# Linear attention and a tanh-shrink MLP on one core: the key sums spread over DRAM, and the last denominators on VectorE

## The chip, the cores and the metric

The kernel runs on one core of a Trainium2 chip. The metric is the device time of one execution in microseconds (us). Three runs of the kernel before took 283.5, 283.87 and 283.98 us; the median is 283.87 us.

The core has five engines that run beside each other and meet at semaphores: TensorE (PE, with its weight loads shown as PEld), VectorE (DVE), ScalarE (ACT), GpSimd (POOL) and SyncE (SP, which here only issues transfers). Each engine works through its own instructions in the order in which the program issued them. Transfers (DMA) are issued by SP or by POOL and are moved by 16 DMA engines.

## The reference: what is computed

There are 8 batches, 8 heads, 576 tokens and 64 numbers per head. All arrays are float32.

```
phi(x) = where(x > 0, x, exp(x) - 1) + 1
kv  = sum over tokens of phi(k) v        (64 x 64 for each batch and head)
z   = sum over tokens of phi(k)          (64 numbers for each batch and head)
num = phi(q) kv
den = phi(q) . z + 1e-6
x   = num / den                          -> 4608 tokens x 512
h   = x w_in                             (512 x 2048)
g   = h - tanh(h)
out = g w_out                            (2048 x 512)
```

## The kernel before, in words

**Chunks.** The MLP runs over nine chunks `c` of 512 tokens. Chunk 0 to 7 holds the first 512 tokens (eight of nine groups of 64) of batch `c`; chunk 8 holds the ninth group of all batches, the "last tokens". A chunk has two parts. In the first (`l1mm`, L458) 16 steps `fi` of 4 matmuls make h, into PSUM bank `fi % 6`; after every odd step ACT takes tanh of two banks (`l1act2`, L464) and DVE subtracts it from h into `gT` (L465), which frees the two banks. So step 6 of a chunk can't write bank 0 before the DVE subtraction of steps 0 and 1 is done. In the second part (`l2mm`, L479) 16 steps `s` of 4 matmuls make the output, four steps for 128 tokens; ACT copies each result to one of five `osb` buffers (L490), and SP stores it in two or four transfers (L503).

**Attention in the gaps.** While chunk `c` is computed, the attention of the batches `n1 = c + 1` and `n2 = c + 2` is prepared. The order is written out by hand: `s1[i]` lists what is issued after step `i` of the first part, `s2[i]` what is issued after step `i` of the second part. What is in a list is put into the engines' queues at that place, whether its inputs are ready or not.

**Batches 3 to 7** (`n2 >= QS`) take this way. In `s2` of chunk `c`, ACT and DVE make phi(k) and phi(q) of batch n2. At `s2[9]` (`s2[12]` in chunk 1) `a_num` computes the numerators of batch n1 and then, with 72 small matmuls (L198), kv and z of batch n2. z comes out with one number on each of 128 partitions (two heads of 64) for four pairs of heads. It is needed the other way round: all 64 numbers along the free dimension, on all partitions. For this `kz_copy` has DVE copy z, repeated 64 times, to `zr` (L218); two steps later `q_zb` multiplies `zr` with the identity on PE (L227, two matmuls), and ACT copies the product to `zb` (L230). POOL multiplies phi(q) with `zb` in two halves `i` (`q_prod`, L237), and DVE sums each half and head (`q_den`, L242, four reductions): the first half is summed at `s2[15]` of the same chunk (in chunk 2 at `s1[2]` for batch 3), the second at `s1[3]` and `s1[5]` of the next. At `s1[7]` `q_scale` adds 1e-6 and inverts on DVE, POOL scales phi(q) (L251), and SP issues a transposing transfer (L170) whose result `a_num` uses.

**The last tokens of batches 0 and 1** are left out of the load of q in those batches. They are loaded in chunk 3 (`load_qr`), go through phi in chunk 4 (`r_phi`, which also issues their transposition, L327), and at `s2[9]` of chunk 6 `r_den` makes their denominators on PE (L335), DVE inverts them (L338, L340), SP takes them through DRAM to all partitions (L343, L347), and `r_num` makes the numerators on PE (L288). In chunk 7 `r_scale` divides on DVE (L359).

**Loads.** `load_k`, `load_q` and `load_v` of the batch after n2 are issued by POOL at `s2[9]` (in chunk 1 at `s2[15]`), in this order; k and q have one buffer each, v has two.

Of the kernel before, what the change touches and what calls it, by code (L numbers as in the profile page):

```python
# [18 lines left out]
def kernel(  # L19
# [115 lines left out]
    zr_t, zb_t, pr_t, dn_t, r_t = {}, {}, {}, {}, {}  # L135
# [76 lines left out]
    def kz_copy(b, b0, o):  # L212
        ps = ps_all[:, b0:b0 + 2, o:o + 132].rearrange("p g (i e) -> p g i e", i=2)
        if b < QS:
            nc.vector.tensor_mul(kz_t[b][:, :, :, 64:96], ps[:, :, :, 64:65].to_broadcast([128, 2, 2, 32]), mask)
        else:
            zr_t[b] = rpool.tile([128, 2, 2, 64], BF16, name="zr")
            nc.vector.tensor_copy(zr_t[b].rearrange("p i g t -> p g i t"),  # L218
                                  ps[:, :, :, 64:65].to_broadcast([128, 2, 2, 64]))
        nc.vector.tensor_copy(kz_t[b][:, :, :, 0:64], ps[:, :, :, 0:64])  # L220


    def q_zb(b, bank):

        ps = ps_all[:, bank, 0:256]
        for i in range(2):
            nc.tensor.matmul(ps[:, 128 * i:128 * i + 128], zr_t[b][:, i].rearrange("p g t -> p (g t)"), ident,  # L227
                             start=True, stop=True)
        zb_t[b] = rpool.tile([128, 2, 128], BF16, name="zb")
        nc.scalar.copy(zb_t[b].rearrange("p i x -> p (i x)"), ps)  # L230
# [87 lines left out]
    def r_phi():  # L318
# [6 lines left out]
        nc.vector.tensor_tensor(y, e, r, ALU.min)  # L325
        qT_t["r"] = const.tile([128, 2, 2, 2, 64], BF16, name="qTr")
        nc.sync.dma_start_transpose(out=qT_t["r"].rearrange("p b i g t -> p (b i) (g t)"), in_=y)  # L327

    def r_den(bank, o):

        qT = qT_t["r"]
        ps = ps_all[0:64, bank, o:o + 64]
        for n, p in enumerate((0, 2, 1, 3)):
            for b in range(2):
                nc.tensor.matmul(ps[32 * b:32 * b + 32], kz_t[b][:, p // 2, p % 2, 64:96], qT[:, b, p % 2, p // 2, :],  # L335
                                 start=(n == 0), stop=(n == NP - 1))
        den = const.tile([64, 64], F32, name="denr")
        nc.vector.tensor_scalar(den, ps, 1e-6, None, ALU.add)  # L338
        rden = const.tile([64, 64], F32, name="rdenr")
        nc.vector.reciprocal(rden, den)  # L340
        ds = dram.tile([2, H, 64], F32, name="dsr")
        for b in range(2):
            nc.sync.dma_start(out=ds[b], in_=rden[32 * b:32 * b + H])  # L343
        rdb = rdb_t["r"] = const.tile([128, 2, NP, 64], F32, name="rdbr")
        for b in range(2):
            for hh in range(2):
                nc.sync.dma_start(  # L347
                    out=rdb[64 * hh:64 * hh + 64, b].rearrange("p a t -> p (a t)"),
                    in_=ds[b, 4 * hh:4 * hh + 4].rearrange("a t -> (a t)").partition_broadcast(64))

    def r_num(b0, o):

        pr_t["r"] = [rest_mm(b, b0, o + 128 * b, qT_t["r"][:, b].unsqueeze(2)) for b in range(2)]

    def r_scale():

        for b in range(2):
            for h, ps in enumerate(pr_t["r"][b]):
                nc.vector.tensor_mul(xT[:, 2 * h:2 * h + 2, rest_at(b):rest_at(b) + 64], ps,  # L359
                                     rdb_t["r"][:, b, 2 * h:2 * h + 2])  # L360
# [123 lines left out]
    def evac(c, i, o, f0=0, f1=None):  # L484
# [145 lines left out]
    for c in range(NC):  # L630
# [4 lines left out]
        if c == 0:  # L635
# [44 lines left out]
            def k2(i):  # L680
                ks.append(phi_pieces(2, k_t, kp_t, "kp", i))
                ks[i][1]()
# [3 lines left out]
        elif n1 < B:  # L686
            if c == 1:
# [15 lines left out]
            if c == 3:  # L703
                s1[12].append(load_qr)
            if c == 4:
                s2[1].append(r_phi)
            if c == B - 2:
                s2[m].append(lambda: (r_den(7, 384), r_num(6, 128)))
            s2[m].append(lambda: a_num(n1, n2 if n2 < B else 0))
            if n2 < B:  # L710
                s2[m + 2].append(lambda: (q_zb(n2, 4 if c == 1 else 7), q_prod(n2)))
                if c > 1:
                    s2[15].append(lambda: (q_den(n2, 0, 0), q_den(n2, 0, 1)))
        if c == B - 1:
            s1[3].append(r_scale)
        if c == 1:
            for i in range(2):
                s1[1 + 2 * i].append(lambda i=i: ks[i][0]())
                s1[3 + 2 * i].append(lambda i=i: ks[i][2]())
            s1[0].append(lambda: (a_vp(2, 0, nc.gpsimd), a_vp(2, 1, nc.gpsimd),  # L720
                                  gate(qT_t[n1]), load_k(n2), load_q(n2), load_v(n2)))
        if c >= 1 and n2 < B:
# [7 lines left out]
            if n2 + 1 < B:  # L730
                s2[15 if c == 1 else 9].append(lambda: (load_k(n2 + 1), load_q(n2 + 1), load_v(n2 + 1)))
# [91 lines left out]
```

## Time and profile before

| | |
|---|---|
| median of three runs | 283.87 us |
| the profiled execution's own time | 283.29 us |
| its span, first to last instruction | 281.5 us |
| PE busy | 276.1 us, 98% of the span |
| DVE, ACT, POOL busy | 176.9, 146.0, 81.9 us |
| granted TensorE clock | 1.00 |
| transfers | 33.25 MB in 40135 packets, mean 118 GB/s |

Busy time is the time in which an engine worked on instructions. The chain is the work that ended last, followed back from the last instruction: each piece of it is what the next one waited for. What stands on the chain costs time, and what does not stand on it is covered. Of the chain 91% is PE, above all the two big matmul lines L458 (43%) and L479 (41%).

### The profile page before, as it was taken

The numbers are of one execution on the slowest core, as the hardware profiler recorded it, in microseconds if no ns is written. First come the engines' busy times: TensorE is split into PE (matmuls) and PEld (weight loads), VectorE is DVE, ScalarE is ACT, GpSimd is POOL, SyncE is SP. The second block draws the span as 40 slices with busy tenths as digits, with TensorE's granted clock in tenths as the row PEclk, the third lists the DMA queues.
The fourth block names the chain that finished last, engine by engine and source line by source line (L and its number), as shares of the span: only waits on it lengthen the run. The fifth ranks groups of instructions, "written<-read, shape, count | busy, mean of one in ns | idle before, by whom it ended". The sixth has DMA issues, their size and how long they took to land.

```text
span 281.5 us, 5103 instructions
## 1 busy us (share of the span) xinstructions
PE 276.1 (98%) x2085; PEld 131.0 (47%) x2085; DVE 176.9 (63%) x285; ACT 146.0 (52%) x177; POOL 81.9 (29%) x79
## 2 busy tenths in 40 slices
PE   8899999999999999999999999999999999999995
PEld 3574544444544454445444544454444444444443
DVE  5759967993879755976398839763961177006600
ACT  4747918856255654675357636673541365126411
POOL 8642330320092434362623361406050000000000
PEclk9999999999999999999999999999999999999999
DMA  6999999799829899079904990342025210230023
GB/s 102 189 205 207 205 207 206 158 196 213 228 46 204 117 199 214 1 123 161 207 18 96 173 222 18 73 90 67 8 43 118 77 36 2 51 78 20 2 66 83
DMA packets 40135, 33.25 MB, mean 118 GB/s; under 512 B 17744, under 2 KB 35824, under 8 KB 39984
## 3 DMA queue, kind: packets, MB, share of 16 engines
q0 software_dynamic: 18688, 18.35, 41.5%
q1 hardware_dynamic: 21424, 14.58, 21.9%
q8 instruction: 16, 0.26, 0.3%
q14 instruction: 7, 0.06, 0.0%
HBM read 38.14 MB, written 9.46 MB: 169 GB/s over the span
## 4 chain that ended last, share of the span: by engine, by line
PE 91%; DMA 4%; DVE 1%; ACT 1%; issue 1%; POOL 1%; SPq 0%; DVEq 0%; POOLq 0%
PE ps_all L458 43%; PE ps_all L479 41%; DMA out_dram<-osb 3%; DMA kraw<-in_k_dram 2%; PE ps_all L198 2%; PE ps_all L742 1%; PE ps_all L279 1%; ACT osb L490 1%; SPq L503 0%; PE ps_all L309 0%; POOL qraw L101 0%; ACT e L151 0%; PE ps_all L182 0%; PE ps_all L371 0%; DVE rden L380 0%
## 5 line engine op out<-in xcount | busy, mean ns | idle before, releaser
L479 PE MATMUL ps_all<-w_out_sb,gT 128*128 128x512 bf16 x560 | 124.6, 379 | 0.0
L458 PE MATMUL ps_all<-xT,w_in_sb 128*128 128x512 bf16 x560 | 122.8, 379 | 0.0
L465 DVE TENSOR_TENSOR gT<-ps_all,th 128x1024 bf16<-128x1024 f32 x64 | 77.7, 1217 | 45.2 <-ACT th L464 45.2
L464 ACT ACTIVATE th<-ps_all 128x1024 f32<-128x1024 f32 x64 | 65.6, 1024 | 46.7 <-PE ps_all L458 46.7
L458 PEld LDWEIGHTS <-w_in_sb 128*128 128x128 bf16 x560 | 54.6, 98 | 65.7 <-issue 0.3
L479 PEld LDWEIGHTS <-gT 128*128 128x128 bf16 x560 | 53.8, 98 | 63.2 <-issue 0.2
L490 ACT COPY osb<-ps_all 128x512 f32<-128x512 f32 (+1 forms) x36 | 20.7, 582 | 56.9 <-PE ps_all L479 46.3
L237 POOL TENSOR_TENSOR pr<-qp,zb 128x1152 f32<-128x1152 bf16 x10 | 23.4, 2359 | 37.8 <-ACT zb L230 37.8
L251 POOL TENSOR_TENSOR qp<-qp,rd 128x1152 bf16<-128x1152 bf16 x10 | 21.0, 2115 | 36.9 <-issue 23.7
L242 DVE TENSOR_REDUCE dn<-pr 128x9 f32<-128x576 f32 x20 | 14.5, 746 | 12.2 <-POOL pr L237 12.2
L151 ACT ACTIVATE e<-qraw 128x1152 bf16<-128x1152 bf16 (+1 forms) x16 | 18.2, 1135 | 3.6 <-DMA qraw<-in_q_dram 3.6
L151 ACT ACTIVATE e<-kraw 128x1152 bf16<-128x1152 bf16 x15 | 17.5, 1165 | 0.0
L153 DVE TENSOR_TENSOR kp<-e,r 128x1152 bf16<-128x1152 bf16 x15 | 11.9, 792 | 4.1 <-ACT e L151 3.2
L153 DVE TENSOR_TENSOR qp<-e,r 128x1152 bf16<-128x1152 bf16 (+1 forms) x16 | 11.9, 742 | 4.0 <-ACT e L151 3.0
L568 PE MATMUL ps_all<-zero 128*128 128x512 bf16 x29 | 9.2, 475 | 1.2 <-DVE zero L513 1.2
L124 POOL DMA_DIRECT2D w_out_sb<-in_moe_w_out_dram x10 | 6.4, 637 | 10.1 <-DMA w_in_sb<-in_moe_w_in_dram 4.7
L104 POOL DMA_DIRECT2D kraw<-in_k_dram x7 | 5.5, 783 | 11.0 <-ACT e L151 10.6
L202 DVE COPY vp<-v 128x1152 bf16<-128x1152 bf16 x11 | 6.0, 542 | 4.0 <-DMA v<-in_v_dram 4.0
L470 DVE TENSOR_TENSOR gT<-ps_all,th 128x512 bf16<-128x512 f32 x12 | 7.9, 686 | 0.6
L104 POOL DMA_DIRECT2D qraw<-in_q_dram x7 | 5.3, 752 | 9.9 <-ACT e L151 5.2
L469 ACT ACTIVATE th<-ps_all 128x512 f32<-128x512 f32 x12 | 7.2, 596 | 1.9 <-DVE gT L748 1.0
L420 ACT CAST xT<-ps_all 128x1024 bf16<-128x1024 f32 x5 | 5.1, 1012 | 5.1 <-PE ps_all L288 4.4
(108 smaller groups left out, 146.8 us busy)
## 6 DMA issues: line engine op xcount, KB each, us to landing
out_dram<-osb SPq DMA_DIRECT2D x65, 128.0 KB, 2.4
kraw<-in_k_dram POOLq DMA_DIRECT2D x7, 576.0 KB, 7.0
qraw<-in_q_dram POOLq DMA_DIRECT2D x6, 576.0 KB, 8.7
v<-in_v_dram POOLq DMA_DIRECT2D x6, 576.0 KB, 12.4
w_in_sb<-in_moe_w_in_dram POOLq DMA_DIRECT2D x3, 512.0 KB, 9.8
v<-in_v_dram POOLq DMA_DIRECT2D x4, 288.0 KB, 8.7
rdb<-ds SPq DMA_DIRECT2D x2, 576.0 KB, 5.7
w_out_sb<-in_moe_w_out_dram POOLq DMA_DIRECT2D x4, 256.0 KB, 11.7
```

The costliest lines, as they stand in the source:

```text
L104: nc.gpsimd.dma_start(out=t[:, :, :, 0:n].rearrange("q h i j d -> q (h i) (j d)"), in_=x.rearrange("(n q) x -> q n x", n=4))
L151: return (lambda: nc.scalar.activation(e, x, AF.Exp), lambda: nc.vector.tensor_scalar(r, x, 0.0, 1.0, ALU.max, ALU.add), lambda: nc.vector ...
L153: lambda: nc.vector.tensor_tensor(y, e, r, ALU.min))
L237: nc.gpsimd.tensor_mul(pr_t[b][:, i].rearrange("p j h d -> p j (h d)"), qp_t[b][:, i].rearrange("p j h d -> p j (h d)"), zb_t[b][:, i].uns ...
L242: nc.vector.tensor_reduce(dn_t[b][:, i, :, h], pr_t[b][:, i, :, h, :], mybir.AxisListType.X, ALU.add)
L251: nc.gpsimd.tensor_mul(x, x, rd[:, i].unsqueeze(2).to_broadcast([128, J * 2, D]))
L458: nc.tensor.matmul(h, w_in_sb[:, p, fi * 128:(fi + 1) * 128], xT[:, p, c * 512:(c + 1) * 512], start=(n == 0), stop=(n == NP - 1))
L464: nc.scalar.activation(th, h, AF.Tanh)
L465: nc.vector.tensor_sub(gT[:, fi:fi + 2, :], h, th)
L479: nc.tensor.matmul(o, gT[:, fi, i * 128:(i + 1) * 128], w_out_sb[:, fi, :], start=(fi == 0), stop=(fi == NF - 1))
L490: nc.scalar.copy(osb[:, f0:f1], o[:, f0:f1])
L568: nc.tensor.matmul(ps_all[:, 0, :], zero[:, 0:128], zero, start=True, stop=True)
```

## The change

For batches 3 to 7 `zr` and the two matmuls are gone. DVE copies z as it is (four numbers a partition) to `zs`, and the new `z_rows` has SP store them to DRAM, turned round, and load them back to 128 partitions by two transfers, each to 64 partitions; these three transfers are issued by `kz_copy`, two steps before the place where `q_zb` stood. The reductions of the first half go to `s1[0]` and `s1[1]` of the next chunk (`s1[2]` and `s1[3]` in chunk 2).

For the last tokens of batches 0 and 1, z is taken from the masked columns of `kz_t` by a maximum (`r_z`, chunk 3) and goes through `z_rows` too; in chunk 4 (`r_scale`) DVE multiplies, sums, inverts and scales phi(q) before its transposition. `r_den` and the transfers of its result are gone, `r_num` writes the finished numbers, and `r_copy` copies them.

Besides: the second half of batch 2's r piece (`ks[1][1]`) moves from the end of chunk 0 to `s1[5]` of chunk 1; `kv2` and `a_den` of batch 2 go one step later; v is loaded before q; and only one instead of five of the output stores of chunk 3 is cut in two.

```diff
         if b < QS:
             nc.vector.tensor_mul(kz_t[b][:, :, :, 64:96], ps[:, :, :, 64:65].to_broadcast([128, 2, 2, 32]), mask)
         else:
-            zr_t[b] = rpool.tile([128, 2, 2, 64], BF16, name="zr")
-            nc.vector.tensor_copy(zr_t[b].rearrange("p i g t -> p g i t"),
-                                  ps[:, :, :, 64:65].to_broadcast([128, 2, 2, 64]))
+            zs = rpool.tile([128, 1, 2, 2], BF16, name="zs")
+            nc.vector.tensor_copy(zs[:, 0], ps[:, :, :, 64])
+            zb_t[b] = z_rows(zs, rpool, "zb")[:, 0]
         nc.vector.tensor_copy(kz_t[b][:, :, :, 0:64], ps[:, :, :, 0:64])
-    def q_zb(b, bank):
-        ps = ps_all[:, bank, 0:256]
-        for i in range(2):
-            nc.tensor.matmul(ps[:, 128 * i:128 * i + 128], zr_t[b][:, i].rearrange("p g t -> p (g t)"), ident,
-                             start=True, stop=True)
-        zb_t[b] = rpool.tile([128, 2, 128], BF16, name="zb")
-        nc.scalar.copy(zb_t[b].rearrange("p i x -> p (i x)"), ps)
+    def z_rows(zs, pool, name):
+        nb = zs.shape[1]
+        zd = dram.tile([nb, 2, 2, 128], BF16, name="zd" + name)
+        nc.sync.dma_start(out=zd.rearrange("n g i x -> x (n g i)"), in_=zs.rearrange("x n g i -> x (n g i)"))
+        zb = pool.tile([128, nb, 2, 128], BF16, name=name)
+        for g in range(2):
+            nc.sync.dma_start(out=zb[64 * g:64 * g + 64].rearrange("p n i x -> p n (i x)"),
+                              in_=zd[:, g].rearrange("n i x -> n (i x)").partition_broadcast(64))
+        return zb
...
+    def r_z():
+        zs = const.tile([128, 2, 2, 2], BF16, name="zsr")
+        for b in range(2):
+            nc.vector.tensor_reduce(zs[:, b], kz_t[b][:, :, :, 64:72], mybir.AxisListType.X, ALU.max)
+        zb_t["r"] = z_rows(zs, const, "zbr")
+    def r_scale():
+        y = qp_t["r"]
+        pr = const.tile([128, 8, D], F32, name="prr")
+        nc.vector.tensor_mul(pr.rearrange("p n d -> p (n d)"), y, zb_t["r"].rearrange("p b i x -> p (b i x)"))
+        dn = const.tile([128, 8], F32, name="dnr")
+        nc.vector.tensor_reduce(dn, pr, mybir.AxisListType.X, ALU.add)
+        nc.vector.tensor_scalar(dn, dn, 1e-6, None, ALU.add)
+        rd = const.tile([128, 8], F32, name="rdr")
+        nc.vector.reciprocal(rd, dn)
+        x = y.rearrange("p (n d) -> p n d", d=D)
+        nc.vector.tensor_mul(x, x, rd.unsqueeze(2).to_broadcast([128, 8, D]))
         qT_t["r"] = const.tile([128, 2, 2, 2, 64], BF16, name="qTr")
         nc.sync.dma_start_transpose(out=qT_t["r"].rearrange("p b i g t -> p (b i) (g t)"), in_=y)
-    def r_den(bank, o):
...
     def r_num(b0, o):
-        pr_t["r"] = [rest_mm(b, b0, o + 128 * b, qT_t["r"][:, b].unsqueeze(2)) for b in range(2)]
-    def r_scale():
...
+        for b in range(2):
+            rest_mm(b, b0, o + 128 * b, qT_t["r"][:, b].unsqueeze(2))
+    def r_copy(b0, o):
+        for h, copy in enumerate((nc.vector.tensor_copy, nc.scalar.copy)):
+            copy(xT[:, 2 * h:2 * h + 2, rest_at(0):rest_at(2)].rearrange("p i (b t) -> p b i t", b=2),
+                 ps_all[:, b0 + h, o:o + 256].rearrange("p (b i t) -> p b i t", b=2, i=2))
...
-                cuts = [f0, 256, f1] if c == 3 and 2 * i + half > 2 else [f0, f1]
+                cuts = [f0, 256, f1] if c == 3 and 2 * i + half > 6 else [f0, f1]
...
                 ks.append(phi_pieces(2, k_t, kp_t, "kp", i))
-                ks[i][1]()
+                if not i:
+                    ks[i][1]()
...
-                s1[10].append(kv2)
+                s1[11].append(kv2)
-                s1[12].append(lambda: (a_den(n1, 6), a_spread(n1)))
+                s1[13].append(lambda: (a_den(n1, 6), a_spread(n1)))
-                if c == 2:
-                    s1[2].append(lambda: (q_den(n1, 0, 0), q_den(n1, 0, 1)))
                 e = 2 * (c == 2)
+                for h in range(2):
+                    s1[e + h].append(lambda h=h: q_den(n1, 0, h))
...
+                s2[13].append(r_z)
             if c == 4:
                 s2[1].append(r_phi)
-            if c == B - 2:
-                s2[m].append(lambda: (r_den(7, 384), r_num(6, 128)))
-            s2[m].append(lambda: a_num(n1, n2 if n2 < B else 0))
+                s2[12].append(r_scale)
+            s2[m].append(lambda: (c == B - 2 and r_num(6, 128), a_num(n1, n2 if n2 < B else 0),
+                                  c == B - 2 and r_copy(6, 128)))
             if n2 < B:
-                s2[m + 2].append(lambda: (q_zb(n2, 4 if c == 1 else 7), q_prod(n2)))
-                if c > 1:
-                    s2[15].append(lambda: (q_den(n2, 0, 0), q_den(n2, 0, 1)))
-        if c == B - 1:
-            s1[3].append(r_scale)
+                s2[m + 2].append(lambda: q_prod(n2))
...
-                s1[3 + 2 * i].append(lambda i=i: ks[i][2]())
+                s1[3 + 2 * i].append(lambda i=i: (i and ks[i][1](), ks[i][2]()))
...
-                s2[15 if c == 1 else 9].append(lambda: (load_k(n2 + 1), load_q(n2 + 1), load_v(n2 + 1)))
+                s2[15 if c == 1 else 9].append(lambda: (load_k(n2 + 1), load_v(n2 + 1), load_q(n2 + 1)))
```

More of the change, by code (lines that the diff above doesn't have):

```diff
@@ L134 @@
     kp_t, qp_t, qT_t, kz_t, rdb_t, rden_t = {}, {}, {}, {}, {}, {}
-    zr_t, zb_t, pr_t, dn_t, r_t = {}, {}, {}, {}, {}
+    zb_t, pr_t, dn_t, r_t = {}, {}, {}, {}
     def phi_pieces(b, src, store, name, i, parts=0):
@@ L325, in r_phi @@
         nc.vector.tensor_tensor(y, e, r, ALU.min)
+        qp_t["r"] = y
+    def r_z():
[14 more added lines that the diff above has]
+        nc.vector.tensor_mul(x, x, rd.unsqueeze(2).to_broadcast([128, 8, D]))
@@ L326, in r_phi @@
         qT_t["r"] = const.tile([128, 2, 2, 2, 64], BF16, name="qTr")
         nc.sync.dma_start_transpose(out=qT_t["r"].rearrange("p b i g t -> p (b i) (g t)"), in_=y)
-    def r_den(bank, o):
[L331 to L341, printed above, removed]
-        for b in range(2):
[L343 to L349, printed above, removed]
@@ L351, in r_num @@
-    def r_num(b0, o):
-        pr_t["r"] = [rest_mm(b, b0, o + 128 * b, qT_t["r"][:, b].unsqueeze(2)) for b in range(2)]
-    def r_scale():
[L357 to L360, printed above, removed]
+    def r_num(b0, o):
+        for b in range(2):
+            rest_mm(b, b0, o + 128 * b, qT_t["r"][:, b].unsqueeze(2))
```

## The prediction

> **What bounds the kernel now.** I read the page's busy times first, then the chain in order of time, then the timeline around one batch's z, then SP's own waits, and last the transfers of that stretch.
>
> ```profile
> PE 276.1 (98%) x2085; PEld 131.0 (47%) x2085; DVE 176.9 (63%) x285; ACT 146.0 (52%) x177; POOL 81.9 (29%) x79
> ```
>
> PE has no slack. The chain shows what the change can take off it:
>
> ```profile
> 100.86 0.64 PE ps_all L198 x72
> 101.50 1.83 PE ps_all L479 x8
> 103.34 0.11 PE ps_all L227 x2
> 103.45 3.45 PE ps_all L479 x16
> 106.90 13.81 PE ps_all L458 x64
> ...
> 216.75 0.24 PE ps_all L335 x8
> 216.99 0.02 issue
> 217.01 0.23 DVE denr L338
> 217.24 0.04 issue
> 217.28 0.32 PE ps_all L288 x15
> ```
>
> The columns are start, duration, what. L227 (z spread by matmul) costs 0.11 us a batch. At 216.75 eight matmuls make r_den, and then PE waits 0.29 us for DVE to read them. L458 runs at 13.81/64 = 0.216 us a matmul, so a step of four takes 0.863.
>
> Chunk 2's timeline (start, duration, engine, line; in brackets the idle time before and what ended it):
>
> ```profile
> 101.57 0.42 DVE L218 CAST zr<-ps_all 128x256 bf16<-128x256 f32 x1 [0.58 <-PE ps_all L198]
> ...
> 103.86 0.38 ACT L230 CAST zb<-ps_all 128x256 bf16<-128x256 f32 x1
> 104.32 4.68 POOL L237 TENSOR_TENSOR pr<-qp,zb 128x1152 f32<-128x1152 bf16 x2 [2.34 <-ACT zb L230]
> 106.71 1.42 DVE L242 TENSOR_REDUCE dn<-pr 128x9 f32<-128x576 f32 x2 [3.05 <-POOL pr L237]
> ...
> 109.72 1.23 DVE L465 TENSOR_TENSOR gT<-ps_all,th 128x1024 bf16<-128x1024 f32 x1 [1.60 <-ACT th L464]
> ```
>
> DVE already stands 3.05 us for POOL's product, but before it is needed for gT; 1.60 us of idle time are left after the sums. Whatever makes zb later first eats that cover and then holds gT, the PSUM banks and PE.
>
> SP's waits for the two trips through DRAM that the kernel has (total, times, longest), and the transfers issued from 98 to 103 us and from 103 to 107 us (us to landing last):
>
> ```profile
> SPq L403 <- DMA ds<-rden: 3.7, 1, 3.7
> ...
> SPq L347 <- DMA dsr<-rdenr: 0.6, 1, 0.6
> ```
>
> ```profile
> qraw<-in_q_dram POOLq DMA_DIRECT2D x1, 576.0 KB, 8.6
> v<-in_v_dram POOLq DMA_DIRECT2D x1, 576.0 KB, 12.3
> ```
>
> ```profile
> out_dram<-osb SPq DMA_DIRECT2D x2, 128.0 KB, 6.3
> ```
>
> A few KB to DRAM kept SP 3.7 us when batch loads were under way (L403, 67.5 us) and 0.6 us when none were (L347, 219 us). An output store lands after 2.2 us at the least, but after 6.3 us here beside q and v. In chunks 2, 3 and 4 the loads run over just the place where z now takes its trip; in chunk 5 there are none, and in chunk 1 they are issued later.
>
> **The change, part by part.**
>
> *PE work removed.* Five times L227: 5 x 0.11 = 0.55. r_den 0.24 and the wait behind it 0.29: 0.53. Together 1.08 us off the chain; nothing is added on PE.
>
> *z through DRAM, chunks 2 to 5.* How late may zb be? z is out of PSUM at 101.57 + 0.2 (estimate; the 64-element DVE read L338 took 0.22) = 101.77. L458 begins at 106.79 (0.11 earlier), and its step 6 wants bank 0 after 6 x 0.863 = 5.18, at 111.97. DVE now has one reduction (L242, 0.74) queued ahead of the first gT (1.22); with 0.1 to release PE, POOL's first half must end by 109.9. It takes 2.36 + 0.08, so zb must be there by 107.5: the trip may take 5.7 us.
>
> The trip: the store, 0.1 for SP's wait, 0.53 until the second load's issue (L347's own spacing), and that load's landing. Without loads under way: store 2.4 (64 rows of 2 KB; lowest 1.24, from dsr's issue at 217.84 to L347 at 219.08; highest 4.7, a qT transposition, which is also made of small pieces), load 2.5 (rdbr). Sum 5.5: inside 5.7, so chunk 5 costs 0, up to 2.1 by the highest.
>
> With loads under way (chunks 2, 3, 4): the lowest store is ds, issued at 63.34 and waited for until 67.52, 4.2; the highest is 7.7, the maximum of the output stores. I take 4.7, near ds, which carries as little, with 0.5 for 512 separate pieces of 2 bytes instead of 8 rows. For the load the ends are 2.5 (the batch loads are through by then) and 5.7 (rdb); I take 3.5, because v now starts some 3 us earlier and the queue is nearly empty five us after the store. Trip 4.7 + 0.1 + 0.53 + 3.5 = 8.8, stall 8.8 - 5.7 = 3.1 each, 9.3 for three. The ends: 4.2 and 2.5 give 7.3, stall 1.6, 4.8 in all; 7.7 and 5.7 give 14.0, 8.3 each, 25 in all.
>
> *Chunk 1 (batch 3).* z is ready at 75.4; the first sum stands at s1[2], behind gT of steps 0 and 1, so the limit is step 8: 77.69 + 6.9 = 84.6, less 1.22 + 0.74 + 0.1 + 2.44 gives zb by 80.1, a trip of 4.7. The output stores of 73.54 and 74.05 are still in front (3.5 each); store 2.9, so 2.9 + 0.1 + 0.53 + 2.5 = 6.0: stall 1.3 (0 to 3).
>
> *What queues behind.* SP: 18 transfers come, 6 of r_den's go, and 4 cuts go. While SP waits for a store it holds the output stores issued after s2[11]; five osb buffers, refilled every 4 steps (3.45), cover that, and ACT waits for osb only in the last chunk. POOL: q_prod waits for zb; behind it stand q_scale's products, which sat idle 7.9 us before (L251), and in chunk 1 batch 4's loads, some 4 us later, with k wanted at 94. The transposition, issued at 121.12 and landed 5.5 later, was 2.7 us ahead of its use at 129.35. All these I cost at 0; if a cover is short, the next thing late is qT, and with it a_num.
>
> *Last tokens.* r_z is two reductions of some 0.16 (L617) in chunk 3. r_scale is 0.7 + 0.75 + 0.17 + 0.3 + 0.7, about 2.6 on DVE (L153, L242, L246, L248), in chunk 4 at s2[12], where DVE stood 3.05 for POOL: hidden, and its z is a chunk old. Its transposition took SP 1.23 and moves about 10 us later, still nearly two chunks ahead of use. r_copy, about 0.4 each on DVE and ACT, lies before a DVE idle of 6.76 (226.25); four L359 of 0.28 go from chunk 7. All 0, since none is on the chain and these idles cover them.
>
> *Batch 2.* kv2 one step later puts kz_copy behind one more gT; before, kz was ready about when a_den began (59.47), and I reckon 0.4 (0 to 0.9) of PE wait. rdb also comes one step later, toward the multiply at 75.94: inside that 0.4. The half r piece (0.46) only changes place on DVE.
>
> *Sum.* -1.08 + 9.3 + 0 + 1.3 + 0.4 = +9.9 us. The profiled execution's own time was 283.29 (span 281.5 and 1.8 around it), so it would be 293.2; the median of the three runs lies 0.58 higher, and I give the forecast on it: 283.87 + 9.9 = 293.8.
>
> **Two rules of the Trainium skill weighed.** The rows give 2.2 to 7.7 us for a store. "DMA: Bandwidth & Descriptors", section "Anatomy of one DMA", makes a small transfer cost about 2.0 us fixed; two in a row would be 4.0 plus issue, inside the limit, and the sum would be no stall. The rows of this case under load contradict it, so I go by them. The granted clock is 1.00 in every chunk here. "TensorE: Matmul & The Clock Gate", section "What's actually happening", halves the clock after an idle window of about 3.4 us; by that rule stalls of 3.1 would add nothing, longer ones up to some 1.7 each, about 5 for three.
>
> **Rivals.**
>
> *In time after all (faster).* SP's packets pass the batch loads: a trip under load of 5.7 or less costs nothing. For it: ds was issued as 4 transfers behind 4 slow output stores, so its 4.2 may be queue, not load. Against it: even 4.2 + 0.63 + 2.5 is 7.3. Price: -1.08 + 0 to 0.4, 282.8 to 283.2. It turns at 5.7 us.
>
> *Pieces take turns (much slower).* Each DMA engine writes 512/16 = 32 pieces; if each lets one packet of a batch load pass (1152 B; about 0.1 us: the transfers view counts some 340 packets of the loads between 105 and 107 us, on 16 engines), a store takes 3.4 more, the three stalls 6.5 each: +20 instead of +9.3, about 304.
>
> *The trip is hidden for most batches.* One stall remains: about 284 to 287.
>
> **How the numbers follow.** Forecast (three stalls) 0.65, own range 288 to 301 from the trip's ends, cut where both ends would have to meet in every batch. In time 0.18, of which 0.16 is below 283.3. Pieces take turns 0.11. One stall or less 0.06, half of it within 0.2%. So faster 0.16, same 0.06, slower 0.78, where 0.2% (0.57 us) is about what a measurement tells from no change. The range, 282.7 to 301, must reach down to the first rival to leave no more than 2 in 10 out.
>
> **What would show it.** Right: a new PE idle before step 6 of chunks 3, 4 and 5, ended by DVE gT; DVE L242 waiting for POOL pr some 6 us instead of 3; POOL waiting for a DMA into zb; no such idle in chunk 6. Wrong: zb landing within 5.7 us under load, or the sums' wait staying inside idle time. The prediction fails most easily in the landing time of a 512-piece store beside the batch loads, which no row shows.

## The result, and the profile after

The changed kernel takes 367.09 us (median of six runs, 365.72 to 370.12), beside 283.76 us for the kernel before, run next to it (six runs, 283.5 to 284.4). The ratio is 1.295, with a 95% interval of 1.290 to 1.300: 83.3 us more. The forecast was 293.8 us, its range 282.7 to 301. The direction was right and the size far out. The profiled execution took 365.72 us, its span is 363.9 us, and its mean granted clock 0.906. Runs more than 1.5% above the fastest run of the same kernel count as slow and are left out of the times and ratios below, three of four of "z by matmul" and two of five of "busy stall", whose traces are of slow runs.

The page of the kernel after, engines, slices and granted clock:

```profile
PE 281.4 (77%) x2037; PEld 132.3 (36%) x2067; DVE 177.7 (49%) x287; ACT 144.7 (40%) x173; POOL 82.3 (23%) x79
...
PE   8899999985089930999309975089952999999996
...
PEclk9999999999579995899858999579995899999999
```

The work is nearly the same as before, on every engine. PE's idle time went from 281.5 - 276.1 = 5.4 us to 363.9 - 281.4 = 82.5 us, and the slices show where: five holes of one to two slices (9.1 us each), and in each of them and just behind it a lower clock.

The waits of the kernel after (engine, line, what it waited for: us in total, times, longest):

```profile
POOL pr L238 <- DMA zb<-zdzb: 131.2, 5, 38.5
DVE dn L243 <- POOL pr L238: 94.3, 5, 22.3
...
PE ps_all L458 <- DVE gT L465: 69.5, 5, 15.6
...
PE ps_all L280 <- DMA qT<-qp: 2.6, 1, 2.6
```

Read from the top, this is the path the prediction named: POOL's product waits for `zb`, the reduction L243 waits for POOL, `gT` stands behind the reduction on DVE, and PE stands for `gT`. But the last link costs 69.5 us and not 10.6 (9.3 and 1.3). The chain of the kernel after gives one whole turn of it, from chunk 2 into chunk 3 (start, us, what):

```profile
120.11 17.44 DMA zdzb<-zs
137.62 3.39 DMA zb<-zdzb
141.00 0.62 issue
141.62 2.36 POOL pr L238
144.01 0.75 DVE dn L243
144.76 1.14 DVE gT L465
145.94 1.01 PE ps_all L458 x2
```

One KB on its way to DRAM takes 17.44 us, 32 KB back to 64 partitions 3.39. The same store has no load to compete with in chunk 5, and is still on the chain with 13.60. That chunk's timeline (start, us, engine, line; in brackets the idle time before and what ended it):

```profile
258.35 0.40 SPq L226 DMA_DIRECT2D zdzb<-zs  x1
...
271.96 1.12 SPq L229 DMA_DIRECT2D zb<-zdzb  x2
...
275.23 4.69 POOL L238 TENSOR_TENSOR pr<-qp,zb 128x1152 f32<-128x1152 bf16 x2 [26.77 <-DMA zb<-zdzb]
277.62 0.76 DVE L243 TENSOR_REDUCE dn<-pr 128x9 f32<-128x576 f32 x1 [17.64 <-POOL pr L238]
...
279.56 1.01 PE L458 MATMUL ps_all<-xT,w_in_sb 128*128 128x512 bf16 x2 [11.00 <-DVE gT L465]
```

The transfers of the kernel after (out<-in, queue, times, KB each, median us from issue to landing) have it for all of them; `zdzbr` is the trip of the last tokens:

```profile
zb<-zdzb SPq DMA_DIRECT2D x10, 32.0 KB, 3.4
...
zdzb<-zs SPq DMA_DIRECT2D x5, 1.0 KB, 17.2
zdzbr<-zsr SPq DMA_DIRECT2D x1, 2.0 KB, 16.0
```

So the load behaves as expected and the store doesn't. Why it takes 13 to 17 us, and how much of the 83 us hangs on that, is what the runs had to settle.

### The profile page after: what moved, and what is told of

It is laid out like the page before. It is cut to its first block, busy times and chain, and to the rows that moved or that the text cites. A ratio compares the mean times of both kernels' runs of the same rounds, so it can differ in the third digit from the quotient of the medians.

```text
span 363.9 us, 5043 instructions
## 1 busy us (share of the span) xinstructions
PE 281.4 (77%) x2037; PEld 132.3 (36%) x2067; DVE 177.7 (49%) x287; ACT 144.7 (40%) x173; POOL 82.3 (23%) x79
## 4 chain that ended last, share of the span: by engine, by line
DMA 44%; PE 40%; DVE 5%; POOL 3%; ACT 3%; SPq 2%; issue 2%; POOLq 0%; ACTq 0%
DMA zdzb<-zs 22%; PE ps_all L458 19%; PE ps_all L479 19%; DMA zdzbr<-zsr 4%; DMA v<-in_v_dram 4%; DMA qraw<-in_q_dram 4%; DMA zb<-zdzb 3%; DVE gT L465 3%; DMA w_in_sb<-in_moe_w_in_dram 3%; POOL pr L238 3%; DMA qT<-qp 2%; DMA out_dram<-osb 2%; ACT e L151 1%; SPq L503 1%; SPq L229 1%
## 5 line engine op out<-in xcount | busy, mean ns | idle before, releaser
L458 PE MATMUL ps_all<-xT,w_in_sb 128*128 128x512 bf16 x550 | 130.6, 395 | 72.2 <-DVE gT L465 69.5
L479 PE MATMUL ps_all<-w_out_sb,gT 128*128 128x512 bf16 x541 | 121.8, 379 | 1.7 <-issue 1.1
L458 PEld LDWEIGHTS <-w_in_sb 128*128 128x128 bf16 x560 | 56.5, 101 | 144.2 <-issue 84.5
L243 DVE TENSOR_REDUCE dn<-pr 128x9 f32<-128x576 f32 x20 | 14.9, 747 | 94.3 <-POOL pr L238 94.3
L151 ACT ACTIVATE e<-kraw 128x1152 bf16<-128x1152 bf16 x15 | 17.4, 1163 | 0.0
L153 DVE TENSOR_TENSOR kp<-e,r 128x1152 bf16<-128x1152 bf16 x15 | 11.9, 797 | 4.0 <-ACT e L151 3.1
L153 DVE TENSOR_TENSOR qp<-e,r 128x1152 bf16<-128x1152 bf16 (+1 forms) x16 | 11.9, 742 | 4.0 <-ACT e L151 3.0
L420 DVE CAST xT<-ps_all 128x1024 bf16<-128x1024 f32 x5 | 6.1, 1217 | 7.0 <-PE ps_all L289 7.0
## 6 DMA issues: line engine op xcount, KB each, us to landing
qraw<-in_q_dram POOLq DMA_DIRECT2D x6, 576.0 KB, 13.8
```

The source lines that it names most:

```text
L151: return (lambda: nc.scalar.activation(e, x, AF.Exp), lambda: nc.vector.tensor_scalar(r, x, 0.0, 1.0, ALU.max, ALU.add), lambda: nc.vector ...
L153: lambda: nc.vector.tensor_tensor(y, e, r, ALU.min))
L243: nc.vector.tensor_reduce(dn_t[b][:, i, :, h], pr_t[b][:, i, :, h, :], mybir.AxisListType.X, ALU.add)
L420: copy(xT[:, 2 * h:2 * h + 2, m:m + 512], ps_all[:, 2 * h:2 * h + 2, :])
L458: nc.tensor.matmul(h, w_in_sb[:, p, fi * 128:(fi + 1) * 128], xT[:, p, c * 512:(c + 1) * 512], start=(n == 0), stop=(n == NP - 1))
L479: nc.tensor.matmul(o, gT[:, fi, i * 128:(i + 1) * 128], w_out_sb[:, fi, :], start=(fi == 0), stop=(fi == NF - 1))
```

## The experiments

Two theories of the store stood against each other. The first counts: a transfer pays for each of its 512 writes of 2 bytes. The second looks at where they go: "turned round" means that neighbouring partitions write neighbouring 2 bytes, and pieces that share a short stretch of DRAM wait for each other. Beside them stood the question whether the store is the whole of the loss.

### The store by itself

```diff
+    trip(f"turned{r}", [4, 128], lambda d: d.rearrange("y x -> x y"), z4, ...)
+    trip(f"rows{r}", [128, 4], lambda d: d, z4, ...)
+    trip(f"one{r}", [1, 128], lambda d: d.rearrange("y x -> x y"), chain[:, 0:1], ...)
+    trip(f"apart64{r}", [4, 128, 32], lambda d: d[:, :, 0:1].rearrange("y x o -> x y o"), ...)
+    trip(f"apart512{r}", [4, 128, 256], lambda d: d[:, :, 0:1].rearrange("y x o -> x y o"), ...)
+    trip(f"wide64{r}", [4, 128, 32], lambda d: d.rearrange("y x o -> x y o"), ...)
+    trip(f"four{r}", [4, 128], lambda d: d, chain[0:4, 0:128], ...)
```

> The store by itself, without the kernel: transfers one after the other, each issued when the one before has landed, no loads. 512 pieces of 2 bytes turned round as in the change; 128 rows of 8 bytes; 128 pieces of 2 bytes; 512 pieces of 2 bytes each into its own 64 or its own 512 bytes of DRAM; 512 pieces of 64 and of 256 bytes; 4 rows of 256 bytes; 512 pieces of 2 bytes from SBUF to SBUF; the transposition of 128 x 256. Theory A1 (each small write to DRAM is completed before the next of its engine, some 0.37 us each): turned about 13 us, one about 4.5, apart 64 and 512 also 13, wide 256 well under. Theory A2 (writes into the same 64 bytes wait for each other): turned 13, apart 64 or 512 about 2.5 to 4. Either way rows, four, SBUF to SBUF and transposition about 2 to 3.

The transfers of this kernel, with nothing else under way:

```profile
zdapart<-chain SPq DMA_DIRECT2D x4, 1.0 KB, 1.8
...
zdturned<-chain SPq DMA_DIRECT2D x2, 1.0 KB, 12.8
...
zdrows<-chain SPq DMA_DIRECT2D x2, 1.0 KB, 3.0
...
zdone<-chain SPq DMA_DIRECT2D x2, 0.2 KB, 16.0
...
sb<-chain SPq DMA_DIRECT2D x2, 1.0 KB, 2.0
```

`zdturned` is the store of the change: 12.8 us alone, so competition is not needed. `zdapart` writes the same 512 pieces of 2 bytes, 64 or 512 bytes apart, in 1.8 us. `zdone` has a quarter of the pieces, side by side, and takes longer. Four rows of 256 bytes (`four`) took 1.1, and 512 pieces of 64 or 256 bytes (`wide`) 1.8 to 1.9. The first theory falls. It is not the source either: the same four numbers a partition written to SBUF (`sb`) take 2.0.

### How near is too near

```diff
+    for step in (2, 4, 8, 16, 32):                       # 4, 8, 16, 32, 64 bytes apart
+        trip(f"step{step}x{r}", [4, 128, step], lambda d: d[:, :, 0:1].rearrange("y x o -> x y o"), ...)
+    for n in (4, 16):                                    # each partition its own 64 bytes, n pieces of 2 bytes in it
+        trip(f"own{n}x{r}", [128, 1, 32], lambda d: d[:, 0, 0:n], ...)
+    trip(f"turned{r}", [4, 128, 1], ...)                 # 512 pieces side by side
+    trip(f"half{r}", [2, 128, 1], ...)                   # 256
+    trip(f"eight{r}", [8, 128, 1], ...)                  # 1024
```

> The store by itself again, no kernel around it. 512 pieces of 2 bytes with 4, 8, 16, 32 and 64 bytes from one to the next; 128 times 4 and 128 times 16 pieces of 2 bytes, where each partition's pieces lie in 64 bytes of its own; and 256, 512 and 1024 pieces side by side. In the first measurement 512 pieces side by side took 12.8 to 14.3 us, the same pieces 64 or 512 bytes apart 1.8 to 2.0, and 128 pieces side by side 16. Theory A2 (pieces in the same 64 bytes wait for each other, some 0.4 us each): 32, 16, 8, 4, 2 and 1 pieces share 64 bytes at steps of 2, 4, 8, 16, 32 and 64 bytes, so 13, 7, 4, 2.5, 2 and 2 us; the own ones 3 and 8; the number of pieces side by side hardly matters. If the stretch is larger than 64 bytes, the times at 32 and 64 differ; if smaller, those at 16 and 32 are equal.

The transfers of this kernel (the trace puts `zd` before each name, so `own4` stands as `zdown4`):

```profile
zdstep2x<-chain SPq DMA_DIRECT2D x2, 1.0 KB, 8.6
...
zdstep4x<-chain SPq DMA_DIRECT2D x2, 1.0 KB, 4.1
...
zdstep8x<-chain SPq DMA_DIRECT2D x2, 1.0 KB, 2.7
...
zdstep16x<-chain SPq DMA_DIRECT2D x2, 1.0 KB, 2.0
...
zdstep32x<-chain SPq DMA_DIRECT2D x2, 1.0 KB, 1.9
...
zdown4x<-chain SPq DMA_DIRECT2D x2, 1.0 KB, 3.4
...
zdown16x<-chain SPq DMA_DIRECT2D x2, 4.0 KB, 12.3
...
zdturned<-chain SPq DMA_DIRECT2D x2, 1.0 KB, 13.4
...
zdhalf<-chain SPq DMA_DIRECT2D x2, 0.5 KB, 14.3
...
zdeight<-chain SPq DMA_DIRECT2D x2, 2.0 KB, 13.8
```

256, 512 and 1024 pieces side by side take about the same time (13.4 to 14.3 us, and 128 pieces, `zdone` above, 16.0), so it looks as if the stretches are worked on beside each other and only the pieces within one take turns. Counted by pieces that fall into the same 32 bytes the rows fall into one order: 16 pieces 12.3 to 16.0 us, 8 pieces 8.6, 4 pieces 3.4 to 4.1, 2 pieces 2.7, one piece 1.9 to 2.0. It makes no great difference whether the pieces of a stretch come from neighbouring partitions (`step4`, 4.1) or from one (`own4`, 3.4). That is 0.5 to 1.0 us for each further piece in the stretch. Counted by 64 bytes the order breaks: `step2` and `own16` both have 16 pieces there, and take 8.6 and 12.3 (though `own16` has four times as many pieces in all). So 32 bytes fits better, and from a spacing of 32 bytes on the time hardly falls (2.0 and 1.9); it isn't proved. What in the path to DRAM makes such writes take turns no run shows.

### The change with whole rows, and with each piece in its own 64 bytes

Two ways to take the sharing out of the changed kernel, for the most part or wholly, and to keep everything else. The first doesn't turn z round: each partition stores its four numbers as 8 bytes, so that only four rows and not 16 pieces lie in 32 bytes, and `zb` holds its numbers in another order.

```diff
-        zd = dram.tile([nb, 2, 2, 128], BF16, name="zd" + name)
-        nc.sync.dma_start(out=zd.rearrange("n g i x -> x (n g i)"), in_=zs.rearrange("x n g i -> x (n g i)"))
+        zd = dram.tile([128, nb * 4], BF16, name="zd" + name)
+        nc.sync.dma_start(out=zd, in_=zs.rearrange("x n g i -> x (n g i)"))
+        zf = zd.rearrange("(g x) y -> g (x y)", g=2)
...
-                              in_=zd[:, g].rearrange("n i x -> n (i x)").partition_broadcast(64))
+                              in_=zf[g].partition_broadcast(64))
```

> The changed kernel, but z is stored in 128 rows of 8 bytes, not turned round, so that zb holds the right numbers in the wrong order (the turning round is left out; the amount of bytes, the number of transfers, their order and the waits are the same). Theory A (the pieces are what is slow): the store lands in 2.5 to 6 us, the trip takes 6 to 10 us, stalls of 0 to 4 us in five chunks, 287 to 300 us. Rival C (any trip through DRAM beside the loads is this slow): the store stays above 13 us and the time above 350.

It took 310.25 us (309.11 and 311.4), ratio 1.094 (1.089 to 1.098), 10 us above the top of what was expected. Its chain has the stores of chunks 1 to 5; those of 1, 2, 3 and 5:

```profile
75.88 6.26 DMA zdzb<-zs
...
109.58 6.63 DMA zdzb<-zs
...
142.88 7.76 DMA zdzb<-zs
...
214.98 2.83 DMA zdzb<-zs
```

Beside the loads of k, q and v, and in chunk 1 beside output stores and `rdb`, the store takes 6.3 to 7.8 us; in chunk 5, where no loads run, 2.83 (3.0 by itself, `zdrows` above). That the 13 us need no loads and the last 4 us do is seen by laying these rows beside 17.44 and 13.60. The whole trips, from the store's issue to the second load's landing, were 9.5, 9.7, 10.9, 10.5 and 6.1 us, and PE's waits for `gT` fell from 69.5 us to these:

```profile
PE ps_all L459 <- DVE gT L466: 15.7, 5, 5.2
```

The span grew by 25.8 us against the kernel before. Besides those 15.7 us, 2.1 are a wait for `qT`, 1.4 waits for `xT` at chunk 2's start, and 3.6 longer busy time of PE.

The second keeps 512 pieces of 2 bytes, turned round as in the change, but gives each its own 64 bytes. The loads then fetch as many bytes as before without picking z out of them.

```diff
+    zd_of = {nb: dram.tile([4 * nb, 128, 32], BF16, name=f"zd{nb}") for nb in (1, 2)}
...
+        nc.sync.dma_start(out=zd[:, :, 0:1].rearrange("y x o -> x y o"),
+                          in_=zs.rearrange("x n g i -> x (n g i)").unsqueeze(2))
...
+                              in_=zd[g].rearrange("x o -> (x o)")[0:nb * 256].partition_broadcast(64))
```

> The changed kernel, but each of the 512 pieces of 2 bytes goes into 64 bytes of its own in DRAM, and the two loads take as many bytes as before from there without picking z out (the turning round is left out, so the denominators are not the reference's). Pieces, transfers, order and waits are those of the changed kernel; 12 small transfers at the start fill the place. Theory A2: the store lands in 2 to 3 us where no loads run and 5 to 8 beside them, as whole rows did, and the time is that of whole rows, 305 to 315 us. Rival A1 (512 pieces are slow wherever they go, once loads run beside them): 340 or more.

It took 313.39 us (313.31 and 313.48), ratio 1.104 (1.098 to 1.110). Its store in the view of the transfers:

```profile
zd<-zs SPq DMA_DIRECT2D x5, 1.0 KB, 5.0
```

(The landing of some of the five is missing in this view. By the chain they took 5.0 us in chunk 1, 8.0 to 8.5 in chunks 2 to 4, beside the loads, and 2.6 in chunk 5.)

The same number and size of writes with 54 us less, inside the expected 305 to 315. The sharing of stretches is shown as the main cause: 367.1 - 313.4 = 53.7 us by this kernel, 367.1 - 310.3 = 56.8 by the one before it. Some 27 to 30 us over the kernel before remain, so the trip through DRAM loses by itself too.

### z by one transposing transfer

The trip cut to one transfer: DVE repeats z 64 times as in the kernel before, and SP transposes it from SBUF to SBUF, for the last tokens too.

```diff
-            zs = rpool.tile([128, 1, 2, 2], BF16, name="zs")
-            nc.vector.tensor_copy(zs[:, 0], ps[:, :, :, 64])
-            zb_t[b] = z_rows(zs, rpool, "zb")[:, 0]
+            zr = rpool.tile([128, 2, 2, 64], BF16, name="zr")
+            nc.vector.tensor_copy(zr.rearrange("p i g t -> p g i t"), ps[:, :, :, 64:65].to_broadcast([128, 2, 2, 64]))
+            zb_t[b] = rpool.tile([128, 2, 128], BF16, name="zb")
+            nc.sync.dma_start_transpose(out=zb_t[b], in_=zr.rearrange("p i g t -> p (i g t)"))
```

> The changed kernel, but without DRAM: VectorE repeats z 64 times as the kernel before did, and one transposing transfer from SBUF to SBUF does what the identity matmul did, for batches 3 to 7 and for the last tokens. 256 packets of 256 bytes; the transposition of the last tokens (512 such packets) landed in 2.5 us. Theory A: landing 2.5 us where no loads run and 4 to 6 beside them, against about 5.2 that the VectorE order allows; stalls of 0 to 1 us in three chunks, so 283 to 286 us. If loads delay small packets of any kind as the pieces: above 300.

It took 292.86 us (290.83 to 294.34), ratio 1.032 (1.028 to 1.035), some 8 us more than expected. The transposition lands after 2.95 us in chunk 5, where no loads run, but after 7.4 to 8.3 in chunks 2 to 4, beside them; the waits of this kernel:

```profile
PE ps_all L455 <- DVE gT L462: 6.5, 3, 2.7
```

Three stalls, in the three chunks where the prediction had put them. So even one transfer beside the loads is later than the 5.7 us that the order of the work allows, and none of the four ways through DMA replaces two matmuls of 0.11 us without loss.

### z by matmul again, the rest of the change kept

```diff
-            zs = rpool.tile([128, 1, 2, 2], BF16, name="zs")
...
+            zr_t[b] = rpool.tile([128, 2, 2, 64], BF16, name="zr")
...
-                s2[m + 2].append(lambda: q_prod(n2))
+                s2[m + 2].append(lambda: (q_zb(n2, 4 if c == 1 else 7), q_prod(n2)))
```

> The changed kernel, but z of batches 3 to 7 goes through the identity matmul again; the last tokens on VectorE, the moved sums, the load order, kv2 and a_den one step later and the single cut store all stay. Theory A (the store of z in 512 pieces of 2 bytes, 13.6 to 17.4 us to landing, holds VectorE and with it TensorE): the five stalls of 11 to 16 us go; what stays is the same kind of store for the last tokens, which holds SP 16 us and made the transposition late in chunk 4 (3.0 us of TensorE wait), and some 2 us in chunk 1. 283.8 + 3.0 + 2.0 - 0.5 (r_den gone) = about 288. Rival B (the moved sums and the new load order cost by themselves): above 300.

It took 293.56 us (one run), 5.6 more than expected and some 10 more than the kernel before; rival B's 300 is not reached by it. The trace is of a run of 299.58 us, so the sizes of its waits needn't be those of the faster run. The five stalls are gone, but one store of the bad kind is left, that of the last tokens, and it holds SP. SP's wait for it, then the timeline of chunk 4:

```profile
SPq L238 <- DMA zdzbr<-zsr: 17.4, 1, 17.4
```

```profile
156.25 1.31 SPq L238 DMA_DIRECT2D zbr<-zdzbr  x2
157.65 1.83 SPq L512 DMA_DIRECT2D out_dram<-osb  x3
159.60 6.90 SPq L170 DMA_TRANSPOSE qT<-qp  x1
...
173.46 1.06 PE L289 MATMUL ps_all<-qT,kz 64*64 64x512 bf16 x8 [11.87 <-DMA qT<-qp]
```

From the wait's end at 156.25 SP first works off the output stores that piled up; the transposition of batch 5's phi(q), which stood behind them, is issued at 159.60, when the next loads run, and lands 13.8 us later. `a_num` waits 11.87 us for it in this run. In the changed kernel the same place shows only 2.6 us (L280 above), where its transposition landed after 7.5 us and not 13.8.

### The last tokens on VectorE alone

Before, with only this part of the change: denominators of the last tokens on DVE, `r_den` and its transfers gone. Their z goes by one transposing transfer in chunk 5 and not by the bad store; two output stores are cut.

```diff
-    def r_den(bank, o):
+    def r_z():
...
+        zb_t["r"] = const.tile([128, 2, 2, 128], BF16, name="zbr")
+        nc.sync.dma_start_transpose(out=zb_t["r"].rearrange("p b i x -> p (b i) x"),
+                                    in_=zr.rearrange("p b i g t -> p (b i g t)"))
+    def r_scale():
...
-            if c == B - 2:
-                s2[m].append(lambda: (r_den(7, 384), r_num(6, 128)))
+            if c == 5:
+                s1[12].append(r_z)
+                s2[12].append(r_scale)
+            s2[m].append(lambda: (c == B - 2 and r_num(6, 128), a_num(n1, n2 if n2 < B else 0),
+                                  c == B - 2 and r_copy(6, 128)))
```

> The kernel before with only the last tokens' denominators on VectorE, and z for them spread by one transposing transfer from SBUF in chunk 5, where no loads run and SP waits for nothing behind it; two instead of five output stores cut. It takes r_den and the wait behind it (0.53 us) off TensorE: 283.2, about 0.5 under the kernel before. Rival (something hidden takes it back: VectorE in chunk 5, or the order of the last stores): 283.7 or more.

283.18 us (twelve runs, 282.8 to 284.25) beside 284.07 (nineteen runs), ratio 0.9967 (0.9953 to 0.9982): 0.9 us (0.5 to 1.3) faster than the kernel before, as expected, and the fastest kernel here. The chain in chunk 6, where before `r_den`'s eight matmuls and 0.29 us of waiting stood:

```profile
209.14 8.63 PE ps_all L484 x40
217.78 0.25 PE ps_all L288 x16
218.03 0.43 PE ps_all L279 x8
```

L484 (the second part) is followed at once by the numerators of the last tokens (L288) and `a_num` (L279): no `r_den` and no wait. The part of the prediction's gain that it priced at 0.53 us is there; what the rest of the 0.9 is was not separated.

### The moves alone

The kernel before with batch 2's r piece, `kv2` and `a_den` one step later, the sums at their new places and v ahead of q.

```diff
-                s1[10].append(kv2)
+                s1[11].append(kv2)
...
-                s1[12].append(lambda: (a_den(n1, 6), a_spread(n1)))
+                s1[13].append(lambda: (a_den(n1, 6), a_spread(n1)))
...
-                s2[15 if c == 1 else 9].append(lambda: (load_k(n2 + 1), load_q(n2 + 1), load_v(n2 + 1)))
+                s2[15 if c == 1 else 9].append(lambda: (load_k(n2 + 1), load_v(n2 + 1), load_q(n2 + 1)))
```

> The kernel before with only what the change moves: the sums of the first half at s1[0] and s1[1], batch 2's r piece, kv2 and a_den one step later, v loaded before q. z by matmul and r_den stay. My working: 0 for all but batch 2 (0.4, and the changed kernel shows 0.8 to 1.1 at a_den and at the first steps of chunk 2): 284.0 to 285.0. Rival (the moves cost several us by themselves): above 287.

285.57 us (eight runs, 284.89 to 285.82) beside 284.07, ratio 1.005 (1.003 to 1.007): 1.5 us more, and 0.6 above the top of what was expected. The timeline at chunk 2's start shows most of it:

```profile
78.37 2.48 DVE L429 TENSOR_TENSOR xT<-ps_all,rdb 128x512 bf16<-128x512 f32 x4 [0.96 <-DMA rdb<-ds]
79.11 0.38 PE L458 MATMUL ps_all<-xT,w_in_sb 128*128 128x512 bf16 x1 [0.72 <-DVE xT L429]
```

`rdb`, one step later, is now late for the multiply that makes chunk 2's input, and PE stands for that: 0.72 us here and 0.4 in two waits that follow, 1.1 of the 1.5.

### Sums late, and a busy PE in the stalls

Two tries at giving back part of the loss in the changed kernel. The first moves the sums behind all `gT` of the first part, so that a late `zb` can't hold them:

```diff
-                    s1[e + h].append(lambda h=h: q_den(n1, 0, h))
-                s1[3 + e].append(lambda: q_den(n1, 1, 0))
-                s1[5 + e].append(lambda: q_den(n1, 1, 1))
-                s1[7 + e].append(lambda: q_scale(n1))
+                    s1[11 + h].append(lambda h=h: q_den(n1, 0, h))
+                s1[13].append(lambda: q_den(n1, 1, 0))
+                s1[14].append(lambda: q_den(n1, 1, 1))
+                s1[15].append(lambda: q_scale(n1))
```

> The changed kernel with the sums of z times phi(q) moved behind the subtractions that TensorE needs: s1[11], s1[12], s1[13], s1[14], and the scaling to s1[15], in all chunks. The trip stays as slow as it is. Theory A (the stall comes about because the sums stand ahead of gT in VectorE's order): the waits of TensorE for gT fall from 11 to 16 us to under 3, and a wait for qT at the numerators takes their place: scaling at about 15.5 us into the chunk, 4.2 on POOL, 5 for the transposition, 25 against 22.4; 3 to 6 us in five chunks, with the last tokens' 12: 300 to 325 us. Rival (SP held by the trip is what delays, through stores or transpositions): above 350.

It took 359.63 us (359.11 and 360.16), ratio 1.266 (1.262 to 1.270): a miss by 35 us and more, in the range that was set for the rival (SP held by the trip). Its waits:

```profile
PE ps_all L280 <- DMA qT<-qp: 33.6, 5, 15.6
PE ps_all L479 <- DVE gT L465: 21.6, 9, 6.1
```

The wait before step 6 is gone and the loss stands one link further on. From the store's issue at 76.71 its chain runs over the load, POOL's product, the sums, POOL's scaling (4.20) and a transposition of 10.69 us to `a_num` at 121.33: 44.6 us, where the kernel before has 29 from one `a_num` to the next. So the path from z's store to `qT` has become longer than a chunk, whatever the order of the sums. The longest wait, 15.6 us, is the rival's kind: in chunk 4 SP was held for 13.6 us by the store of the last tokens, and the transposition behind it took 14.5. This order of issue moved the wait about; it didn't hide it.

The second keeps PE busy with 60 matmuls of zeros at each stall, so that its clock is not lowered:

```diff
+            if 2 <= c <= 6 and fi == (8 if c == 2 else 6):
+                for _ in range(60):
+                    nc.tensor.matmul(ps_all[:, 7, :], zero[:, 0:128], zero, start=True, stop=True)
```

> The changed kernel with 60 matmuls of zeros (60 x 0.216 = 13.0 us), into PSUM bank 7 that nothing reads there, put in front of step 6 of the first part in chunks 3 to 6 and of step 8 in chunk 2, so that TensorE works where it stood. They add work and take nothing away; whatever the time falls by is what the halved clock behind the stalls costs. The profile of the changed kernel shows the clock at 0.5 for 13.7 us in each of five stalls, of which some 3 us reach past the stall. Theory A (the clock costs as well): 5 x 1.5 to 2 = 7 to 10 us less, about 358. Rival (the clock costs nothing, the stalls are all): 367 or a little more.

364.79 us (three runs, 364.24 to 367.02), ratio 1.283 (1.279 to 1.287) beside 1.295 of the changed kernel: about 3.3 us less, 0.7 to 5.9 by the two intervals, where 7 to 10 were expected. The mean granted clock rose from 0.906 to between 0.981 and 0.995. 60 such matmuls take 13.1 us, more than chunk 6's stall of 11.0, so up to 2.1 us of gain may be hidden in that. The lowered clock is a small part of the 83 us.

## Why the prediction was wrong, by its own steps

**The store, 4.7 us for each of three (ends 4.2 to 7.7): wrong, and the main error.** Measured: 16.1 to 17.4 beside loads, 13.6 without. The step priced the transfer "near `ds`, which carries as little", with 0.5 us for 512 pieces instead of 8 rows. Neither bytes nor the number of pieces sets it; pieces side by side do, 16 in the same 32 bytes. No row of the profile before had pieces that share a stretch, so its rows could bound the store only as if it were of their kind, and the upper end was no bound. The text said that the prediction fails most easily here, but gave the range no reach for it.

**Chunk 5 at 0 and chunk 1 at 1.3: wrong by the same step.** The stalls were 11.0 and 14.6, and the sign "no such idle in chunk 6" did not come. With whole rows chunk 5's trip was 6.1 against the 5.5 predicted, and chunk 1's 9.5 against 6.0. Chunk 5's "no loads, no stall" was thus nearly right for a harmless store; chunk 1's was not, for its store met output stores and `rdb` and took 6.3 instead of 2.9.

**The load, 2.5 and 3.5: right.** Measured 2.6 in chunk 5, and 3.4, 3.4, 3.0 and 2.7 in chunks 1 to 4; behind the quicker store of whole rows it was 2.5 to 2.9.

**What the trip may take, 5.7 us: right.** In the changed kernel the chunk 2 trip was 141.0 - 120.1 = 20.9, so the stall should be 15.2; it was 15.6. Chunk 5's was 275.1 - 258.4 = 16.7, so 11.0; it was 11.0. Chunk 1's limit of 4.7 gives 21.1 - 4.7 = 16.4; it was 14.6, behind 1.4 us of waits for `xT` at the chunk's start. The path zb, POOL, DVE's reduction, `gT`, PSUM bank, PE was right link by link, and so was the place, step 6 and in chunk 2 step 8.

**The sum even for a harmless store: too low.** Whole rows gave 310.25 where the prediction's sum was 293.8. The trips beside loads were 9.7 to 10.9 instead of 8.8, because such a store took 6.6 to 7.8, near the upper end and not 4.7; chunk 1's trip is the 9.5 above; and `qT` came 2.1 us late for one `a_num`, which the prediction had costed at 0.

**Last tokens at 0, "its z is a chunk old": wrong.** The z was early enough, and the DVE work was hidden (0.9 us gained in the kernel that has only this part). But SP waited 15.4 us for that store, and behind it stood the transposition of batch 5. The prediction had listed qT as "the next thing late" and asked for it only after a 4.7 us store. Its price was a wait of 2.6 us in the changed kernel, and of 11.9 in the traced run of the one with z by matmul.

**Batch 2's moves at 0.4 (0 to 0.9): too low.** 1.5 us for all the moves together, 1.1 of it `rdb` one step later, the very row the prediction had put "inside that 0.4".

**PE work removed, 1.08: right**, as far as the runs show it: 0.9 us for the last tokens' part and what goes with it. The 0.55 of the five L227 was not measured by itself.

**The clock.** The forecast left it out, with stalls of 3.1 us. The stalls are 11 to 16 us, and the profile after shows a granted clock of 0.50 for 13.7 us at each: it begins 3.0 to 4.8 us into the stall and reaches 2.8 to 2.9 us past its end, 5.7 in chunk 6. A window of the kernel after, from the end of chunk 2's stall (start and end, us, then busy time and count of PE, PEld, DVE, ACT and POOL, granted clock, DMA share, GB/s):

```profile
101.48:104.40 2.92, 2.72 (x6) 0.99 (x7) 2.92 (x4) 1.02 (x1) 2.60 (x4) 0.50 0.30 22
```

Six matmuls take 2.72 us here, 0.45 each instead of 0.216. PE's busy time rose by 5.3 us although 0.79 of its work (0.55 and 0.24) went, so slower matmuls cost some 6 us; the busy stall gave 3.3 back, and up to 2.1 may be hidden. The rule of the Trainium skill, "TensorE: Matmul & The Clock Gate", section "What's actually happening", has the kind of it right: the clock halves after an idle window of about 3.4 us, and 13.7 is four of them. But an idle time shorter than such a window was enough here: in the one-transposition kernel 2.73 us of idle PE were followed by 3.4 us at 0.50, and with whole rows 2.05 us and some small matmuls behind them, while 2.94 us with whole rows were not. So the prediction could not count on stalls of 3.1 us to leave the clock alone.

**The other rule weighed.** By "DMA: Bandwidth & Descriptors", section "Anatomy of one DMA", which is written for transfers that GpSimd issues, such a store would cost about 2.0 us; SP issues it here. The runs show 1.8 to 2.0 for 512 pieces of 2 bytes that lie 32 bytes or more apart, and 12.8 to 14.3 for 256 to 1024 pieces side by side: there the measurement decides.

**The rivals.** "In time after all" and "one stall or less" fell. "Pieces take turns" had named the right object, the 512 pieces, and the wrong thing that they wait for: packets of the batch loads, at 3.4 us a store (by the 345 load packets of that window, 0.093 us each on 16 engines, it would be 3.0). They wait for each other: with no loads at all the store takes 12.8 us.

**Where the 83.3 us are.** By the runs, and as if the parts simply add, 54 to 57 us are the sharing of stretches, the last tokens' store included; 1.5 are the moves, and about -0.9 the last tokens' arithmetic. The rest, 83.3 less 0.6 and less 54 to 57, is 26 to 29 us: the trip through DRAM, mostly beside other transfers, even with a harmless store. That last share is what is left over, and no run measures it by itself. By the trace, 77.1 of the span's 82.4 us more are idle time of PE (69.5 of it the five waits for `gT`), and 5.3 are longer busy time of PE.

## What to carry to other kernels

Before a store of small pieces is priced by bytes or by descriptors, ask which pieces write into the same short stretch of DRAM (32 bytes fits the rows here): keep a partition's numbers together or give each its own stretch, and turn the data round on an engine, as the kernel before does (turning it round on the load was not tried). A transfer that waits on a queue is paid by what stands behind it there, so look for the next transposition or load on that queue and not only for the transfer's own user. And where no row of the profile is of the same kind as the operation, the nearest rows give no upper end; measure the operation by itself first.

## What the runs showed of the hardware that was not expected

- Pieces of 2 bytes in DRAM that share 32 bytes take turns, at 0.5 to 1.0 us each, as far as the times tell: 1.9 us at one piece a stretch, 8.6 at 8, 12.3 to 16.0 at 16, whether there are 128, 256, 512, 1024 or 2048 pieces in all. The same source written to SBUF took 2.0.
- Small transfers issued by SP take more than twice as long beside the batch loads: whole rows 6.6 to 7.8 us against 2.83, a transposition of 128x256 7.4 to 8.3 against 2.95, pieces in their own 64 bytes 8.0 to 8.5 against 2.6. (In chunk 1, beside output stores and `rdb`, the separate pieces took 5.0.)
- The clock of 0.50 outlasts the stall by 2.8 to 5.7 us, but five such tails cost only 3 to 6 of 83 us. An idle time of 2.73 us was followed by 3.4 us at 0.50, one of 2.94 us by none.
